# Weights loaded by pairs of column blocks, state added by VectorE, sums drawn into the sets: three edits to an mLSTM and Fourier-mix kernel

## The chip, the core and the metric

The kernel runs on one core of a Trainium2 chip. Its engines are TensorE (PE; its weight loads are shown apart as PEld), VectorE (DVE), ScalarE (ACT), GpSimd (POOL) and SyncE (SP), whose queue issues all of this kernel's DMAs. Every engine runs its own instructions in the order in which they were written, and waits on semaphores for the others. The metric is device time in microseconds of one execution; the profile is that of one further execution.

## The reference

Two stages follow each other. The first is an mLSTM cell over 4 batches, 8 heads, 768 tokens and head size 40; the second takes its output as x of shape (4, 768, 320), mixes it with a Fourier transform, and puts it through an MLP of width 1280.

```python
for t in range(S):
    m_new = np.maximum(f_gate[:, :, t] + m, i_gate[:, :, t])
    f_stab = np.exp(f_gate[:, :, t] + m - m_new)
    i_stab = np.exp(i_gate[:, :, t] - m_new)
    C = f_stab * C + i_stab * outer(v_t, k_t)
    n = f_stab * n + i_stab * k_t
    y[:, :, t] = sigmoid(o_t) * (C @ q_t) / max(|n . q_t|, 1)
...
u = x + np.real(fft(fft(x, axis=1), axis=2))
un = (u - mean(u)) / sqrt(var(u) + 1e-6)
out = u + np.maximum(un @ w_ch1, 0.0) @ w_ch2
```

The two weight arrays come as float64 and are turned into float32 on the chip.

## The kernel before

**mLSTM.** A batch is cut into 6 chunks of 128 tokens. Within a chunk the recurrence becomes matrix products: scores of keys and queries (`mlstm_scores`, L465, into the two banks `ps`, of which there is one pair), weighed by DVE with a matrix of exponentials (`mlstm_weigh`, L471; ACT makes the exponentials in `mlstm_exp`, L421), then the output of the chunk (`mlstm_from_chunk`, L486) on top of what the state gives (`mlstm_from_state`, L479, from C and the scaled queries qg). The state itself: `mlstm_to_state` (L496) forms what the chunk adds, in the PSUM tile `pc`; `mlstm_decay` (L455, POOL) shrinks the old state with `decB`; `mlstm_gather` puts the new state into `C_next`, and copies the chunk's output to `hT` by ACT (L517 to L528). PE turns that to tokens (`mlstm_turn`, L535), and `mlstm_finish` (L544 to L550, DVE) divides and gates it: x. In batches 1 to 3 the shrunk state lies in `C_next` and DVE adds `pc` to it (L515; a copy, L513, for chunk 0). In batch 0 the shrunk state lies in a tile of its own, `Cd`; PE adds it to `pc` by a product with the identity (L501), and ACT copies the sum (L511). The decays of batch 0 come from DVE (`dec`, L293) by a product (L297) and a copy (L301).

**Mix.** `mix_fold` and `mix_seq` (L695, L698) transform along the tokens, `mix_feat` (L729, into `pu`) along the features, `mix_add` (L749) adds to x, `mix_center` (L765, ACT) subtracts the mean, `mix_turn` (L772, PE, into `put`) turns it, and `mix_turn_out` (L777, ACT) writes the MLP's input `uT`.

**MLP.** The hidden layer has 10 column blocks of 128, two to a step. Batch 0 is plain: `mlp_in` (L837, L841, into `pm`), `mlp_relu` (L850, ACT), `mlp_out` (L943). Batches 1 to 3 use Strassen-Winograd schemes of seven products: `mlp_block` (L897, L902; five blocks of four steps; ACT copies at L915 to L924, DVE adds at L906, relu at L932 and L936) and `mlp_out_pair` (L999; three pairs of token blocks, called sets of four steps), which needs the sums S1 to S4 of hidden blocks (`hidden_sums`, L985, DVE) and adds its results to the output (`residual`, L949, DVE). The two banks x and y of a pair are those that the last adds of `mlp_block`, or the pair before, have just read.

**Weights.** Each of the 10 pieces of 640 columns goes through four steps: `load` (SP, L334, into one of two `raw` buffers), `take` (DVE, L344 and L346: exponent and mantissa), `convert` (ACT, L351 and L352), `join` (DVE, L358 to L364). A load waits until the join of the piece two before has freed its buffer, and what stands behind it in SP's queue waits with it. Of the first weights' five pieces two hold the first 128 input rows (columns 0 to 639 and 640 to 1279), two the last 128 rows, and one, `w1t_sb`, the 64 rows between.

**Order.** Nothing is scheduled by a planner: each step is entered by hand under a slot and a phase, and the steps are written out sorted by both:

```python
def at(slot, phase, fn, *args):
    plan.setdefault((slot, phase), []).append((fn, args))
EVAC, FILL, MAIN, FILL_PE = range(4)
```

Batch 0's mLSTM begins at slot 0 with three slots a chunk, its mix at 22, its MLP at 31; batch 1's mLSTM begins at 32. `when` gives the slots of take, convert and join for each piece, `early` those of the loads.

Of the kernel before, what the change touches and what calls it, by code (L numbers as in the profile page):

```python
# [19 lines left out]
L = 128  # L20
# [30 lines left out]
def kernel(  # L51
# [51 lines left out]
    h_first = const.tile([L, NP, 1], FP, name="h_first")  # L103
    w1_sb = const.tile([L, 2, DFF], FP, name="w1_sb")
    w1t_sb = const.tile([L, DFF // 2], FP, name="w1t_sb")
    w2_sb = const.tile([L, NFF, DM], FP, name="w2_sb")
# [4 lines left out]
    x_bufs = [const.tile([L, NT, DM + 2], FP, name=f"x{n}") for n in range(2)]  # L111

    s_last = const.tile([L, NFF // 2 * L], FP, name="s_last")
    Cd_bufs = [s_last[:, n * NP * D1:(n + 1) * NP * D1].rearrange("p (n m) -> p n m", m=D1) for n in range(2)]
    hT_bufs = [const.tile([L, NP, L], FP, name=f"h{n}") for n in range(2)]
# [6 lines left out]
    def at(slot, phase, fn, *args):  # L122
        plan.setdefault((slot, phase), []).append((fn, args))
# [16 lines left out]
    def gates(gp):  # L140
# [41 lines left out]
        mlstm_load(0, 2)  # L182
        w1_pieces[1].load()
        for t in hT_bufs + Cd_bufs:
            nc.gpsimd.memset(t, 0.0)
# [134 lines left out]
    class Piece:  # L320
# [33 lines left out]
        def join(self):  # L354
# [7 lines left out]
            for d in self.dst:  # L362
# [3 lines left out]

    part = 2 * DM
    w1_pieces = [Piece([w1_sb[:, f // 2, f % 2 * part:(f % 2 + 1) * part]], w_ch1[:, f * part:(f + 1) * part])
                 for f in (0, 2, 1, 3)]
    w1_pieces.insert(2, Piece([w1t_sb], w_ch1[:, 4 * part:]))  # L370
    w2_flat = w_ch2.rearrange("p f m -> p (f m)")
# [74 lines left out]
    def mlstm_decay(b, c):  # L446

        k = chunks[b, c]
        if 0 < c < NT - 1:
            if b == 0:  # L450
                k.Cd = Cd_bufs[c % 2]
            for hip in range(2):
                r, m = slice(hip * 64, hip * 64 + D), slice(hip * 64, hip * 64 + D1)
                d = decB[r, b * NP:(b + 1) * NP, c].unsqueeze(2).to_broadcast([D, NP, D1])
                nc.gpsimd.tensor_tensor(out=k.Cd[r] if b == 0 else k.C_next[r, :, m], in0=k.C[r, :, m], in1=d,  # L455
                                        op=OP.mult)

# [31 lines left out]
    def mlstm_to_state(b, c):  # L489
        k = chunks[b, c]  # L490
        if c < NT - 1:
            add = b == 0 and c > 0
            k.pc = ps_h.tile([L, NP, D1], FP, name="pc", tag="ph")
            for h in range(H):
                r0 = (h % 2) * 64
                nc.tensor.matmul(k.pc[r0:r0 + D, h // 2, :], k.kn[:, h, :], k.vw[:, h, :], start=(h < 2), stop=not add,  # L496
                                 skip_group_check=True)
            if add:
                for hip in range(2):
                    r = slice(hip * 64, hip * 64 + D)  # L500
                    nc.tensor.matmul(k.pc[r], ident[:, r], k.Cd, start=False, stop=True, skip_group_check=True)  # L501

    def mlstm_gather(b, c):
        k = chunks[b, c]
        k.hT = hT_bufs[(b * NT + c) % 2]
        if c < NT - 1:
            for hip in range(2):
                r, m = slice(hip * 64, hip * 64 + D), slice(hip * 64, hip * 64 + D1)
                Cv = k.C_next[r, :, m]
                if b == 0:  # L510
                    nc.scalar.copy(out=Cv, in_=k.pc[r])  # L511
                elif c == 0:
                    nc.vector.tensor_copy(out=Cv, in_=k.pc[r])  # L513
                else:
                    nc.vector.tensor_tensor(out=Cv, in0=Cv, in1=k.pc[r], op=OP.add)  # L515
        if c in BACKWARDS:
            nc.scalar.copy(out=k.hT[:, :, 1:], in_=backwards(k.ph, L - 1, L - 1))  # L517
            if c > TG:
                nc.scalar.copy(out=k.hT[:, :, 0:1], in_=k.ph[:, :, 0:1])
            else:  # L520
                nc.gpsimd.tensor_copy(out=k.hT[:, :, 0:1], in_=h_first)
# [306 lines left out]
    def mlp_in(b, gr, f):  # L828


        k = mixes[b]
        u = [uT_bufs[gr][:, ch].rearrange("p c t -> p (c t)") for ch in range(3)]
        if f % 2 == 0:
            k.pm = [bank("pm", [L, TG * L]) for _ in range(2)]
        for i, ch in ((1, 1),) if f % 2 else ((0, 0), (0, 1), (1, 0)):
            f0 = (f // 2 * 2 + i) * L
            nc.tensor.matmul(k.pm[i], w1_sb[:, ch, f0:f0 + L], u[2 * ch], start=(ch == 0), stop=False)  # L837
        if f % 2:
            for i in range(2):
                r = slice(i * TAIL, (i + 1) * TAIL)  # L840
                nc.tensor.matmul(k.pm[i], w1t_sb[r, f // 2 * L:(f // 2 + 1) * L], u[1][r], start=False, stop=True)  # L841

# [12 lines left out]
    def block(t, n):  # L855
        return t[:, n * L:(n + 1) * L]
# [3 lines left out]
    def weight_sums(n):  # L860

        w = w1_sb.rearrange("p c (n two t) -> p c two n t", two=2, t=L)
        if n == 0:
# [9 lines left out]
        out, x, y, op = ((S3, w[:, 0, 0], w[:, 0, 1], OP.subtract), (w[:, 0, 1], w[:, 0, 1], w[:, 1, 1], OP.add),  # L873
                         (S2, w[:, 0, 1], w[:, 0, 0], OP.subtract), (S4, w[:, 1, 0], S2, OP.subtract))[n]
# [12 lines left out]
    def mlp_block(b, i, step):  # L887
# [5 lines left out]
        T2, T3, T4 = w1x["T"]  # L893
        A = {(r, ch): block(w1_sb[:, ch], f + r) for r in range(2) for ch in range(2)}

# [3 lines left out]
        def tails(gr, banks):  # L899
            for r, bank in enumerate(banks):  # L900
                rows = slice(r * TAIL, (r + 1) * TAIL)
                nc.tensor.matmul(bank, block(w1t_sb, i)[rows], mlp_u(gr, 1)[rows], start=False, stop=True,  # L902
                                 skip_group_check=True)
# [83 lines left out]
    def mlp_out_pair(b, n, step):  # L987
# [8 lines left out]

        def product(po, a, w, start=False):
            for f in range(half):
                nc.tensor.matmul(po, a[:, f], w[:, f], start=start and f == 0, stop=f == half - 1, skip_group_check=True)  # L999
# [4 lines left out]
        if step == 0:  # L1004
            product(x, pair_block(n, 1, 1), w[0, 0], True)
            residual(b, c1, first, x)
            product(y, pair_block(n, 1, 0), w[1, 0], True)
            residual(b, c1, first, y)
# [18 lines left out]
    def plan_mlp(b, s):  # L1027
# [15 lines left out]
        if b > 0:  # L1043
            for j in range(1, 5):
                at(s - 1, FILL + 0.3 if j < 3 else FILL_PE + 0.3, hidden_sums, 0, (j,), 0, NFF // 2 - 1)
            at(s, EVAC, hidden_sums, 0, (1, 2, 3, 4), NFF // 2 - 1, NFF // 2)
        for n in range(TG) if b > 0 else ():
# [63 lines left out]
    for s, load, c in early:  # L1111
# [66 lines left out]
def _pack_w1(w):  # L1178

    t = w[L:L + TAIL].reshape(TAIL, NFF // 2, 2, L).transpose(2, 0, 1, 3).reshape(L, DFF // 2)  # L1180
    return np.ascontiguousarray(np.concatenate([w[0:L], w[L + TAIL:], t], axis=1))

# [45 lines left out]
```

## Time and profile before

| | us |
|---|---|
| median of 3 runs | 422.78 (422.35 to 424.34) |
| profiled execution | 422.23 |
| its span | 420.5 |
| PE busy | 408.1 (97%) |
| DVE busy | 287.5 (68%) |
| ACT busy | 189.6 (45%) |
| POOL busy | 112.0 (27%) |

Times in the text count from the start of the span. A line of the timeline gives start, length, engine, line of the code, operation and tiles (out<-in), how many instructions are merged into it, and in brackets how long the engine had stood idle and what ended that. In the table of waits, a line gives who waited for whom, the sum, how often, and the longest. In the answer on stretches the columns are busy time of PE, PEld, DVE, ACT and POOL, PE's granted clock, the share of the DMA engines and GB/s. The granted clock is 1.00 throughout.

### The profile page before, as it was taken

How to read it: one execution, taken by the hardware profiler on the slowest of the kernel's cores; microseconds unless marked ns; L12 is line 12 of the kernel's file. 1: busy time of each engine (PE TensorE's matmuls, PEld its weight loads, DVE VectorE, ACT ScalarE, POOL GpSimd, SP SyncE). 2: the span in 40 equal slices, each digit the busy share in tenths (PEclk: the TensorE clock that was granted, in tenths of full speed). 3: DMA queues.
4: the chain of work that ended last, by engine and by line, in shares of the span. 5: the costliest groups of instructions: out<-in, count | busy, mean ns of one | idle time of the engine just before them, and what ended most of it. 6: DMA issues, size and time to landing. Idle time of an engine off the chain costs nothing.

```text
span 420.5 us, 7995 instructions
## 1 busy us (share of the span) xinstructions
PE 408.1 (97%) x2966; PEld 301.8 (72%) x2966; DVE 287.5 (68%) x682; ACT 189.6 (45%) x493; POOL 112.0 (27%) x194
## 2 busy tenths in 40 slices
PE   8999999999999999999999999999999999999997
PEld 6877555566567778776559998976459898455996
DVE  8798885767985647778646669778654786325552
ACT  6986375586561232654455423654451123455000
POOL 5554201468332421351221520440300000020000
PEclk9999999999999999999999999999999999999999
DMA  7889297657764254266000543300000000000010
GB/s 228 287 249 335 83 270 234 195 191 203 238 178 146 65 150 145 70 198 215 30 0 2 176 148 124 114 15 1 0 2 0 33 33 32 0 2 0 16 48 31
DMA packets 20549, 47.14 MB, mean 112 GB/s; under 512 B 2784, under 2 KB 9312, under 8 KB 20384
## 3 DMA queue, kind: packets, MB, share of 16 engines
q1 hardware_dynamic: 20512, 46.65, 35.6%
q8 instruction: 23, 0.38, 0.4%
q14 instruction: 14, 0.11, 0.1%
HBM read 42.52 MB, written 4.11 MB: 111 GB/s over the span
## 4 chain that ended last, share of the span: by engine, by line
PE 77%; DVE 12%; DMA 7%; ACT 2%; issue 1%; POOL 0%; SPq 0%; DVEq 0%; ACTq 0%
PE pm L897 17%; PE po L999 16%; PE po L943 8%; PE ps L465 5%; PE pm L902 5%; PE ph L486 5%; PE ph L479 4%; DMA kvt<-in_kv 3%; PE pm L837 3%; PE pu L729 3%; DVE S L985 2%; PE px L535 2%; DMA qk<-in_qkT 2%; PE pz L698 2%; PE put L772 1%; DVE x L949 1%
## 5 line engine op out<-in xcount | busy, mean ns | idle before, releaser
L949 DVE SCALAR_TENSOR_TENSOR x<-po,rstd,x 128x160 f32<-128x160 f32 (+1 forms) x69 | 27.0, 394 | 41.6 <-PE po L999 35.0
L906 DVE TENSOR_TENSOR h<-h,pm 128x384 f32<-128x384 f32 x60 | 30.5, 550 | 33.1 <-ACT h L919 24.7
L421 ACT ACTIVATE W<-W,colT 128x128 f32<-128x128 f32 x144 | 45.0, 395 | 0.0
L443 POOL TENSOR_SCALAR_AFFINE_SELECT W<-W 128x1024 f32<-128x1024 f32 x18 | 21.3, 1185 | 80.8 <-ACT W L421 42.5
L943 PE MATMUL po<-w_sb,h 128*128 128x320 f32 x120 | 34.4, 435 | 0.0
L471 DVE TENSOR_TENSOR W<-ps,W 128x512 f32<-128x512 f32 x48 | 30.7, 680 | 4.5 <-POOL W L443 4.3
L897 PE MATMUL pm<-uT,w_sb 128*128 128x384 f32 x90 | 32.8, 492 | 0.2 <-DVE uT L885 0.2
L837 PE MATMUL pm<-uT,w_sb 128*128 128x384 f32 x80 | 29.9, 501 | 0.7 <-DVE x L749 0.5
L777 ACT COPY uT<-put 128x384 f32<-128x384 f32 x24 | 11.2, 478 | 40.1 <-PE put L772 40.1
L943 PEld LDWEIGHTS po<-w_sb,h 128*128 128x128 f32 x120 | 22.3, 190 | 9.4 <-issue 0.8
L999 PE MATMUL po<-T,S 128*128 128x160 f32 x180 | 27.9, 302 | 0.7 <-DVE x L949 0.6
L465 PE MATMUL ps<-qk 40*128 40x128 f32 x384 | 27.8, 284 | 0.0
L999 PE MATMUL po<-w_sb,h 128*128 128x160 f32 x180 | 26.2, 301 | 1.2 <-DVE h L906 1.2
L999 PEld LDWEIGHTS po<-T,S 128*128 128x128 f32 x180 | 25.5, 190 | 2.6 <-DVE x L949 1.7
L792 POOL TENSOR_TENSOR t<-rstd 128x6 f32<-128x6 f32 x12 | 2.9, 244 | 90.3 <-DVE v L790 89.7
L999 PEld LDWEIGHTS po<-w_sb,h 128*128 128x128 f32 x180 | 24.9, 190 | 2.8 <-DVE h L906 2.4
L465 PEld LDWEIGHTS ps<-qk 40*128 40x128 f32 x384 | 23.4, 188 | 4.1 <-issue 0.7
L486 PE MATMUL ph<-W,kvt 128*41 128x128 f32 x384 | 25.8, 277 | 0.0
L524 ACT COPY h<-ph 41x512 f32<-41x512 f32 (+1 forms) x16 | 9.3, 582 | 35.5 <-PE ph L486 35.4
L431 POOL TENSOR_TENSOR qg<-qk,Gb 128x512 f32<-128x512 f32 x18 | 25.0, 1388 | 0.1
L479 PEld LDWEIGHTS ph<-qg,C 128*128 128x128 f32 x160 | 20.0, 192 | 6.2 <-issue 2.1
L897 PEld LDWEIGHTS pm<-uT,w_sb 128*128 128x128 f32 x90 | 16.2, 190 | 10.8 <-DVE h L906 1.5
(207 smaller groups left out, 862.2 us busy)
## 6 DMA issues: line engine op xcount, KB each, us to landing
W<-M_d SPq DMA_DIRECT2D x18, 512.0 KB
kvt<-in_kv SPq DMA_DIRECT2D x24, 324.0 KB
qk<-in_qkT SPq DMA_DIRECT2D x48, 160.0 KB
raw<-in_w SPq DMA_DIRECT2D x10, 640.0 KB
Gb<-G_d SPq DMA_DIRECT2D x36, 128.0 KB
so<-in_o SPq DMA_DIRECT2D x24, 160.0 KB
out<-x SPq DMA_DIRECT2D x24, 160.0 KB
ds_sb<-in_dft_s SPq DMA_DIRECT2D x1, 1155.0 KB
```

The source lines that it names most:

```text
L421: nc.scalar.activation(out=k.W[:, h, :], in_=M, func=AF.Exp, scale=-1.0, bias=colT[:, c, 0, b * H + h:b * H + h + 1])
L431: nc.gpsimd.tensor_tensor(out=k.qg, in0=k.qk[:, 0], in1=k.Gb, op=OP.mult)
L465: nc.tensor.matmul(k.ps[hip][:, p, :], k.qk[r, 1, p, :], k.qk[r, 0, p, :], start=True, stop=True)
L471: nc.vector.tensor_tensor(out=Wv, in0=k.ps[hip], in1=Wv, op=OP.mult)
L479: nc.tensor.matmul(k.ph[:, p, :], k.C[:, p, :], k.qg[:, p, :], start=(p == 0), stop=False, skip_group_check=True)
L486: nc.tensor.matmul(k.ph[hip * 64:hip * 64 + D1, p, :], k.v1[:, 2 * p + hip, :], k.W[:, 2 * p + hip, :], start=(c == 0 and p == 0), stop=Tr ...
L837: nc.tensor.matmul(k.pm[i], w1_sb[:, ch, f0:f0 + L], u[2 * ch], start=(ch == 0), stop=False)
L897: nc.tensor.matmul(bank, w, u, start=start, stop=True, skip_group_check=True)
L906: nc.vector.tensor_tensor(out=h, in0=h, in1=bank, op=OP.add)
L943: nc.tensor.matmul(k.po, hidden(gr, f)[:, i * L:(i + 1) * L], w2_sb[:, f, :], start=(f == 0), stop=(f == NFF - 1))
L949: nc.vector.scalar_tensor_tensor(out=u, in0=po, scalar=k.rstd[:, c:c + 1], in1=u, op0=OP.mult, op1=OP.add)
L999: nc.tensor.matmul(po, a[:, f], w[:, f], start=start and f == 0, stop=f == half - 1, skip_group_check=True)
```

## The change

Three edits. First, the five pieces of the first weights are cut by pairs of column blocks: piece i holds all input rows for blocks 2i and 2i+1, so that step i of the MLP needs piece i alone. The second piece is loaded at slot 6 and no longer at the start, and the slots of the others move. Second, batch 0's state is kept as in the other batches: POOL shrinks it into `C_next` and DVE adds `pc`; the product with the identity, ACT's copies and the tiles `Cd` go. Third, the sums for the first pair of token blocks are made for three of five hidden blocks while `mlp_block` still runs, and for the other two afterwards, S3 and S4 after the first step of the pair; that step forms four products of x, two of y, the last of x, and the other three of y.

```diff
-    w1_sb = const.tile([L, 2, DFF], FP, name="w1_sb")
-    w1t_sb = const.tile([L, DFF // 2], FP, name="w1t_sb")
+    w1_sb = const.tile([L, NFF // 2, 5, L], FP, name="w1_sb")
...
-    Cd_bufs = [s_last[:, n * NP * D1:(n + 1) * NP * D1].rearrange("p (n m) -> p n m", m=D1) for n in range(2)]
...
-        w1_pieces[1].load()
-        for t in hT_bufs + Cd_bufs:
+        for t in hT_bufs:
             nc.gpsimd.memset(t, 0.0)
...
-    part = 2 * DM
-    w1_pieces = [Piece([w1_sb[:, f // 2, f % 2 * part:(f % 2 + 1) * part]], w_ch1[:, f * part:(f + 1) * part])
-                 for f in (0, 2, 1, 3)]
-    w1_pieces.insert(2, Piece([w1t_sb], w_ch1[:, 4 * part:]))
+    w1_pieces = [Piece([w1_sb[:, i].rearrange("p k t -> p (k t)")], w_ch1[:, i * 5 * L:(i + 1) * 5 * L])
+                 for i in range(NFF // 2)]
...
-            if b == 0:
-                k.Cd = Cd_bufs[c % 2]
...
-                nc.gpsimd.tensor_tensor(out=k.Cd[r] if b == 0 else k.C_next[r, :, m], in0=k.C[r, :, m], in1=d,
-                                        op=OP.mult)
+                nc.gpsimd.tensor_tensor(out=k.C_next[r, :, m], in0=k.C[r, :, m], in1=d, op=OP.mult)
...
-            add = b == 0 and c > 0
             k.pc = ps_h.tile([L, NP, D1], FP, name="pc", tag="ph")
...
-            if add:
-                for hip in range(2):
-                    r = slice(hip * 64, hip * 64 + D)
-                    nc.tensor.matmul(k.pc[r], ident[:, r], k.Cd, start=False, stop=True, skip_group_check=True)
...
-                if b == 0:
-                    nc.scalar.copy(out=Cv, in_=k.pc[r])
-                elif c == 0:
+                if c == 0:
                     nc.vector.tensor_copy(out=Cv, in_=k.pc[r])
                 else:
                     nc.vector.tensor_tensor(out=Cv, in0=Cv, in1=k.pc[r], op=OP.add)
...
-            nc.tensor.matmul(k.pm[i], w1_sb[:, ch, f0:f0 + L], u[2 * ch], start=(ch == 0), stop=False)
+            nc.tensor.matmul(k.pm[i], w1_sb[:, f // 2, 2 * ch + i], u[2 * ch], start=(ch == 0), stop=False)
...
-            product(x, pair_block(n, 1, 1), w[0, 0], True)
+            product(x, pair_block(n, 1, 1), w[0, 0], True, 0, half - 1)
+            product(y, pair_block(n, 1, 0), w[1, 0], True, 0, 2)
+            product(x, pair_block(n, 1, 1), w[0, 0], False, half - 1, half)
             residual(b, c1, first, x)
-            product(y, pair_block(n, 1, 0), w[1, 0], True)
+            product(y, pair_block(n, 1, 0), w[1, 0], False, 2, half)
             residual(b, c1, first, y)
...
-                at(s - 1, FILL + 0.3 if j < 3 else FILL_PE + 0.3, hidden_sums, 0, (j,), 0, NFF // 2 - 1)
-            at(s, EVAC, hidden_sums, 0, (1, 2, 3, 4), NFF // 2 - 1, NFF // 2)
+                at(s - (5, 4, 3, 3)[j - 1], FILL_PE + 0.3, hidden_sums, 0, (j,), 0, NFF // 2 - 2)
+            at(s, EVAC, hidden_sums, 0, (1, 2), NFF // 2 - 2, NFF // 2)
+            at(s, MAIN + 0.1, hidden_sums, 0, (3, 4), NFF // 2 - 2, NFF // 2)
...
-    when = [((2, 0.7), (4, 0.5), (6, 0.6)), ((6, 0.7), (7, 0.5), (8, 0.6)), ((11, 0.7), (13, 0.5), (22, 0.6))]
-    when += [((22, 0.7), (23, 0.7), (27, 0.6)), ((27, 0.7), (28, 0.7), (32, 0.6))]
-    when += [((s, 0.7), (s + 1, 0.7), (s + 2, 0.6)) for s in (33, 36, 39, 42, 45)]
+    when = [((2, 0.7), (4, 0.5), (6, 0.6)), ((11, 0.7), (13, 0.5), (22, 0.6)), ((22, 0.7), (23, 0.7), (27, 0.6)),
+            ((27, 0.7), (28, 0.7), (31, 0.6))]
+    when += [((s, 0.7), (s + 1, 0.7), (s + 2, 0.6)) for s in (31, 34, 37, 40, 43, 46)]
     pieces = w1_pieces + w2_pieces
     for n, (w, p) in enumerate(zip(when, pieces)):
-        if n > 4:
+        if n > 3:
             at(when[n - 2][2][0] + 1, FILL + 0.7, p.load)
...
-             (5, mlstm_load_decay, 4), (6, None, 2), (7, mlstm_load_o, 3), (7, mlstm_load, 5),
-             (11, mlstm_load_decay, 5), (11, None, 3), (11, mlstm_load_o, 4), (12, load_tables, None),
-             (14, mlstm_load_o, 5), (23, None, 4)]
+             (5, mlstm_load_decay, 4), (6, None, 1), (7, mlstm_load_o, 3), (7, mlstm_load, 5),
+             (11, mlstm_load_decay, 5), (11, None, 2), (11, mlstm_load_o, 4), (12, load_tables, None),
+             (14, mlstm_load_o, 5), (23, None, 3)]
```

In `mlp_block` and `weight_sums` only the way in which a block of `w1_sb` is addressed changes; the host's packing of the first weights follows the new cut.

More of the change, by code (lines that the diff above doesn't have):

```diff
@@ L495, in mlstm_to_state @@
                 r0 = (h % 2) * 64
-                nc.tensor.matmul(k.pc[r0:r0 + D, h // 2, :], k.kn[:, h, :], k.vw[:, h, :], start=(h < 2), stop=not add,
+                nc.tensor.matmul(k.pc[r0:r0 + D, h // 2, :], k.kn[:, h, :], k.vw[:, h, :], start=(h < 2), stop=True,
                                  skip_group_check=True)
-            if add:
-                for hip in range(2):
-                    r = slice(hip * 64, hip * 64 + D)
-                    nc.tensor.matmul(k.pc[r], ident[:, r], k.Cd, start=False, stop=True, skip_group_check=True)
     def mlstm_gather(b, c):
@@ L835, in mlp_in @@
         for i, ch in ((1, 1),) if f % 2 else ((0, 0), (0, 1), (1, 0)):
-            f0 = (f // 2 * 2 + i) * L
-            nc.tensor.matmul(k.pm[i], w1_sb[:, ch, f0:f0 + L], u[2 * ch], start=(ch == 0), stop=False)
+            nc.tensor.matmul(k.pm[i], w1_sb[:, f // 2, 2 * ch + i], u[2 * ch], start=(ch == 0), stop=False)
         if f % 2:
@@ L840, in mlp_in @@
                 r = slice(i * TAIL, (i + 1) * TAIL)
-                nc.tensor.matmul(k.pm[i], w1t_sb[r, f // 2 * L:(f // 2 + 1) * L], u[1][r], start=False, stop=True)
+                nc.tensor.matmul(k.pm[i], w1_sb[r, f // 2, 4], u[1][r], start=False, stop=True)
     hid = {}
@@ L860, in weight_sums @@
     def weight_sums(n):
-        w = w1_sb.rearrange("p c (n two t) -> p c two n t", two=2, t=L)
+        A11, A21, A12, A22 = (w1_sb[:, :, j] for j in range(4))
         if n == 0:
@@ L872, in weight_sums @@
         S2, S3, S4 = (view(w1x[t]) for t in ("S2", "S3", "S4"))
-        out, x, y, op = ((S3, w[:, 0, 0], w[:, 0, 1], OP.subtract), (w[:, 0, 1], w[:, 0, 1], w[:, 1, 1], OP.add),
-                         (S2, w[:, 0, 1], w[:, 0, 0], OP.subtract), (S4, w[:, 1, 0], S2, OP.subtract))[n]
+        out, x, y, op = ((S3, A11, A21, OP.subtract), (A21, A21, A22, OP.add), (S2, A21, A11, OP.subtract),
+                         (S4, A12, S2, OP.subtract))[n]
         nc.vector.tensor_tensor(out=out, in0=x, in1=y, op=op)
@@ L893, in mlp_block @@
         T2, T3, T4 = w1x["T"]
-        A = {(r, ch): block(w1_sb[:, ch], f + r) for r in range(2) for ch in range(2)}
+        A = {(r, ch): w1_sb[:, i, 2 * ch + r] for r in range(2) for ch in range(2)}
         def product(bank, w, u, start=False):
@@ L901, in tails @@
                 rows = slice(r * TAIL, (r + 1) * TAIL)
-                nc.tensor.matmul(bank, block(w1t_sb, i)[rows], mlp_u(gr, 1)[rows], start=False, stop=True,
+                nc.tensor.matmul(bank, w1_sb[rows, i, 4], mlp_u(gr, 1)[rows], start=False, stop=True,
                                  skip_group_check=True)
@@ L995, in mlp_out_pair, with product @@
         w = {(r, side): w2_sb[:, 1 - r:NFF:2, side * HALF_D:(side + 1) * HALF_D] for r in range(2) for side in range(2)}
-        def product(po, a, w, start=False):
-            for f in range(half):
+        def product(po, a, w, start=False, f0=0, f1=half):
+            for f in range(f0, f1):
                 nc.tensor.matmul(po, a[:, f], w[:, f], start=start and f == 0, stop=f == half - 1, skip_group_check=True)
@@ L1178, in _pack_w1 @@
 def _pack_w1(w):
-    t = w[L:L + TAIL].reshape(TAIL, NFF // 2, 2, L).transpose(2, 0, 1, 3).reshape(L, DFF // 2)
-    return np.ascontiguousarray(np.concatenate([w[0:L], w[L + TAIL:], t], axis=1))
+    t = w[L:L + TAIL].reshape(TAIL, NFF // 2, 2, L).transpose(2, 0, 1, 3).reshape(L, NFF // 2, L)
+    a, z = (r.reshape(L, NFF // 2, 2 * L) for r in (w[0:L], w[L + TAIL:]))
+    return np.ascontiguousarray(np.concatenate([a, z, t], axis=2).reshape(L, -1))
 def _pack_w2(w):
```

## The prediction

> **What bounds the kernel now.** I read the engine table first, then the waits of all engines, then the timelines of the three places that the diff touches. All times below are the profiled execution's own: span 420.5 us, 422.23 us as timed, 0.55 us under the median of 422.78 us.
>
> ```profile
> PE 408.1 (97%) x2966; PEld 301.8 (72%) x2966; DVE 287.5 (68%) x682; ACT 189.6 (45%) x493; POOL 112.0 (27%) x194
> ```
>
> TensorE (PE) is idle for 12 us in all, so a gain has to be PE work taken out or one of its few waits; a loss is any wait put ahead of PE. Who waits (engine, line, releaser: us, times, longest):
>
> ```profile
> DVE e L344 <- DMA raw<-in_w: 6.4, 2, 5.3
> ...
> PE po L999 <- DVE h L906: 1.2, 2, 0.6
> PE ph L479 <- POOL eo L618: 0.8, 1, 0.8
> ...
> SPq L334 <- DVE m L360: 13.4, 3, 12.5
> ```
>
> PE's own waits are below 1 us each. The other two lines matter more: the queue of loads (SP) once stands still 12.5 us until a weight buffer is free, and VectorE (DVE) once stands 5.3 us for a piece of weights. Today that costs PE nothing. Timeline of that place (start, us, engine):
>
> ```profile
> 49.51 0.33 SPq L334 DMA_DIRECT2D raw<-in_w  x1
> ...
> 59.19 0.53 SPq L334 DMA_DIRECT2D raw<-in_w  x1
> ...
> 61.14 0.87 ACT L850 ACTIVATE h<-pm 128x384 f32<-128x384 f32 x2
> ...
> 63.06 0.61 ACT L765 ACTIVATE uc<-x 128x384 f32<-128x384 f32 x1
> ...
> 63.97 0.49 PE L772 MATMUL put<-ident,uc 128*128 128x128 f32 x3
> ...
> 67.56 0.49 DVE L344 TENSOR_SCALAR e<-raw 128x640 uint32<-128x640 uint32 x1 [5.34 <-DMA raw<-in_w]
> ...
> 68.08 0.83 ACT L351 ACTIVATE e<-e,ebias 128x640 uint32<-128x640 uint32 x1 [3.11 <-DVE e L344]
> ```
>
> The piece issued at 59.19 lands at 67.5. ScalarE (ACT) waits for it too, but only after it has done the relu (L850) and the centering (L765) that PE's transpose at 63.97 needs. The queue was full:
>
> ```profile
> 49.50:67.50 18.00, 17.19 (x80) 9.87 (x78) 11.49 (x23) 11.06 (x24) 1.80 (x2) 1.00 0.95 269
> ```
>
> (last two: DMA share 0.95, 269 GB/s). The other two places:
>
> ```profile
> 37.92 0.48 PE L496 MATMUL pc<-vw,kvt 128*40 128x41 f32 x16
> ...
> 39.49 1.13 PE L479 MATMUL ph<-qg,C 128*128 128x128 f32 x8 [0.81 <-POOL eo L618]
> ...
> 38.43 1.28 DVE L471 TENSOR_TENSOR W<-ps,W 128x512 f32<-128x512 f32 x2
> ...
> 386.78 1.48 DVE L906 TENSOR_TENSOR h<-h,pm 128x384 f32<-128x384 f32 x3
> ...
> 387.38 2.98 PE L999 MATMUL po<-w_sb,h 128*128 128x160 f32 x20 [0.57 <-DVE h L906]
> ...
> 390.74 1.63 PE L999 MATMUL po<-T,S 128*128 128x160 f32 x10 [0.38 <-DVE x L949]
> ```
>
> **Part A, state of the first batch.** Removed: 16 identity records (L501) on PE. From 21.35 to 21.73 such a step takes 0.38, so 4 x 0.38 = 1.5 us. ACT loses its 10 copies (L511, 0.29 each), so its copies of h come 0.6 us earlier and PE's two waits for them at L535 (0.40 and 0.39) go. That is 2.3 us, if nothing else is late. Added on DVE: 10 copies or adds; L513 and L515 show 0.33 and 0.32 for the same shape, about 0.70 a pair. DVE is in order, so their place decides:
>
> - Chunk 0: the pair stands ahead of qg (L429, now 14.65) and dec (L293), and waits until pc (L496) ends at 15.15. It ends at 15.9, qg at 16.5, dec at 16.77 instead of 15.51; PE waits for dec at L297: 16.83 instead of 15.57, +1.26.
> - Chunks 1 to 3: PE makes this up: 1.26 - 3 x 0.38 - 0.79 puts pc of chunk 3 near 32.0 instead of 32.29. DVE now idles for pc (done 32.5), adds until 33.2, and weighs chunk 4 (L471, 1.25) until 34.5. PE, ready at 33.8 for the scores of chunk 5 (L465), needs those buffers: 34.55 against 34.45 before.
> - Chunk 4: behind that weighing stand three finishes (L544 to L550, from 33.16 to 38.43 today, 4.9 to 5.3), the weighing of chunk 5 (1.2) and only then the add of chunk 4 (0.7). 34.5 + 5.1 + 1.2 + 0.7 = 41.5. PE needs that state at L479, today at 39.49: 41.6, **+2.1**.
>
> What follows on PE (L486, L535, then the sequence transform) is back to back, so 2.1 stays; DVE's join before 50 us, and with it the release of SP, moves by the same. Bounds: +0.5, if the three finishes overlap PE's delay better than I place them, to +2.8, with the collision on every finish.
>
> **Part B, weights by pairs.** Pieces are 640 columns as before; one load moves from the start to slot 6, and every later piece is one step behind in number. The piece issued at slot 28 was the sixth, taken at slot 33. It becomes the fifth, with take, convert and join at 31, 32, 33. SP's order before it from slot 23 on is the same, and the hold until the join of slot 22 too, so it lands where the sixth did: at 67.5 (A's shift moves all of it alike and is left out here). New waits: DVE stands at its take from 62.2, as before; behind it are now the join and only then weighing and residual input. ACT stands at its convert, and this convert stands ahead of the first relu pair (L850), four exponentials and the centering (L765). PE's put (L772) waits for the centering:
>
> take 67.56; ACT converts 68.08 to 69.54 (0.83 and 0.72); relu pair to 70.35; exponentials 1.27 to 71.55; centering 0.61 to 72.1. PE's put starts at 72.1 instead of 63.97: **8.2 us** during which PE has nothing else, as its queue is in order.
>
> Second wait: before, the next join stood ahead of the copy of C (L513); now it stands behind it and ahead of the add at L749. After pc near 81.1: copy 0.7, join 2.4, two row copies 0.7, add 0.5: 85.4. PE's product at 76.32, which waits for that add (0.52 today), would be ready at 83.4 and starts at 85.5, 9.2 later than before. So B is **+9.2**. I find no other wait up to 122 us: each weighing is done 1 to 10 us ahead of its scores, and the 0.74 at L479 (109.8) may go or stay. Bounds: 18.0 us x 269/335 (the page's best slice) would land the piece 3.6 earlier, leaving 4.6; without any give-back it is 8.2 + 2.1 = 10.3. I take 9.2, since the same load in the same queue was measured.
>
> [...]
>
> **Part C, sums in the sets.** The four sums (L985) now cover three blocks early and two late, the same elements. Of the early ones S1 and S2, until now ahead of the last three adds (L906, 386.78), move two and more steps up, where DVE waits for ACT's copies (24.7 us of such waits in all). The first add releases PE's first product, so the 0.57 goes, for batch 2 (314.19) and batch 3 (387.38); batch 1 has scores in between and gains nothing. The wait at 390.74 remains: the relus end near 388.65, S1 and S2 for two blocks take some 0.43 each (one block 0.29, four 0.69), the residual 0.38, so PE starts near 390.1: 0.64 in batch 3, 0.57 of it the same wait. In the pairs after, y starts after four instead of five products, 398.57 instead of 398.83, while its bank is free at 398.84: 0.27 waited, but the next step waits for DVE until 400.57 today anyway, so nothing is lost. Sum 0.57 + 0.64 = **-1.2**. Bounds: -1.9, if the other 0.6 of L949 goes too, to +1.6, if all six later pairs lose 0.27.
>
> **Sum.** 422.2 + 2.1 + 9.2 - 1.2 = 432.3 as profiled, 432.9 against the median.
>
> **The rivals.**
> 1. *Faster.* PE work taken out is what counts, and the covers hold: the piece lands by about 61 us, and DVE gets its adds done between other work. Then 422.8 - 1.5 - 0.8 - 1.2 = 419.3. For it: PE is busy 97%, and the first batch is PE's. Against: the measured landing at 67.5, ahead of which there is no slack at all. It decides if the convert ends before PE asks at 63.97, a landing 8 us earlier. 10%.
> 2. *About the same.* Only A and C act: 422.8 + 2.1 - 1.2 = 423.7. For it: in the program before, ACT's wait at 68.08 was harmless. Against: the relu and the centering were ahead of it. 7%.
> 3. *Half.* The load lands at the best rate, 4.6: 428.3. 8%.
> 4. *Sums gain nothing* (what the change says of the sets is not seen by PE): 434.1. Inside the range, counted with the forecast.
> 5. *Worse.* The backlog of joins on DVE reaches the second layer of the first batch, whose weights are all due at 122: one more wait of join and add, 3 to 6 us: 437 to 439. 5%.
>
> **The numbers.** The forecast has 70%. The range goes from rival 3 with A at its low bound (422.8 + 0.5 + 4.6 - 1.9 = 426.0, less the 0.7 of L479: 425.3) to 422.8 + 2.8 + 10.3 + 1.6 = 437.5: 425.3 to 437.0. No change that a measurement of this kernel can tell is about 0.5%, 2.1 us. Faster 0.10 (rival 1), same 0.07 (rival 2), slower 0.83.
>
> **What would show it.** A: no L501, DVE adds with waits for pc, L479 of chunk 5 waiting over 2 us for one. B: PE's put waits about 8 us for the centering, ACT stands at its convert from 61 on with the relu behind it. C: no wait at the first L999 of batches 2 and 3. Wrong if PE has no wait over 3 us before 90 us.

## The result, and the profile after

The changed kernel takes 442.73 us (median of 4 runs, 441.49 to 445.02) where the kernel before takes 422.99 us (422.35 to 424.34) beside it: ratio 1.0469, 95% interval 1.0411 to 1.0526, or +19.8 us. The forecast was 432.9 us, 425.3 to 437.0. The direction was right, and so were the places; the size was half of it. The profiled execution is the longest of the four: 445.02 us, span 443.3, 22.8 more than before.

The engine table of the changed kernel, and TensorE's granted clock in 40 slices of the span (tenths of full speed; before, every slice had a 9):

```profile
PE 417.7 (94%) x2950; PEld 309.2 (70%) x2950; DVE 290.5 (66%) x692; ACT 186.6 (42%) x483; POOL 113.3 (26%) x192
...
PEclk9898997779998999999999999999999999999999
```

TensorE has 16 instructions fewer and is busy 9.6 us longer. The second line says why: the same work was done at a lower clock, 0.50 by the stretches below, in five places. The waits of TensorE (engine, line, releaser: us, times, longest):

```profile
PE put L757 <- ACT uc L750: 10.0, 5, 8.8
PE pm L821 <- DVE x L734: 2.8, 1, 2.8
PE pd L294 <- DVE dec L290: 1.7, 1, 1.7
PE ph L471 <- DVE x L535: 1.6, 1, 1.6
...
PE ph L471 <- POOL qg L426: 1.0, 1, 1.0
PE ph L471 <- DVE C L500: 0.9, 1, 0.9
...
PE po L983 <- DVE x L933: 0.6, 2, 0.3
```

Before, each of TensorE's waits was under 1 us (0.8 at most), apart from the start. Of the new ones those of 8.8, 2.8, 1.7 and 0.9 us were forecast at their places (the last with over 2 us), those of 1.6 and 1.0 us were not, and the wait of `po` for the hidden block that part C was to remove is gone. Timeline of the place with the 8.8 us (start, us, engine, and in brackets the idle time before it and its releaser):

```profile
63.60 0.53 SPq L331 DMA_DIRECT2D raw<-in_w  x1
...
72.37 0.49 DVE L341 TENSOR_SCALAR e<-raw 128x640 uint32<-128x640 uint32 x1 [6.23 <-DMA raw<-in_w]
...
72.90 0.83 ACT L348 ACTIVATE e<-e,ebias 128x640 uint32<-128x640 uint32 x1 [7.95 <-DVE e L341]
...
74.26 0.85 ACT L834 ACTIVATE h<-pm 128x384 f32<-128x384 f32 x2
75.00 1.27 ACT L416 ACTIVATE W<-W,colT 128x128 f32<-128x128 f32 x4
76.17 0.61 ACT L750 ACTIVATE uc<-x 128x384 f32<-128x384 f32 x1
...
76.83 0.90 PE L757 MATMUL put<-ident,uc 128*128 128x128 f32 x3 [8.77 <-ACT uc L750]
...
80.52 2.51 PE L714 MATMUL pu<-dd_sb,Z 128*128 128x321 f32 x4
```

The chain is the one foretold, link by link: the load lands late, ScalarE stands at the convert, and relu, exponentials, centering and `put` stand behind it. What was not foretold is in the durations of the last two lines. Three transposes take 0.90 where they took 0.49, and four products of the feature transform 2.51 where they took 1.35. The stretches of the same execution (bounds, us, then busy us of PE, PEld, DVE, ACT and POOL with their instructions; the last three numbers are the granted clock, the DMA share and GB/s):

```profile
14.81:18.22 3.41, 1.74 (x30) 1.22 (x26) 2.39 (x7) 3.35 (x7) 0.65 (x3) 1.00 0.41 125
18.22:21.63 3.41, 3.41 (x25) 3.06 (x24) 1.89 (x3) 1.99 (x8) 1.49 (x5) 0.50 0.92 258
...
72.40:82.60 10.20, 5.77 (x13) 3.03 (x14) 5.34 (x9) 6.33 (x17) 1.80 (x2) 0.52 0.52 160
82.60:92.90 10.30, 8.46 (x70) 4.80 (x69) 5.08 (x9) 6.22 (x16) 3.10 (x3) 0.98 0.18 52
92.90:99.70 6.80, 5.56 (x10) 2.70 (x12) 3.69 (x9) 2.96 (x7) 2.62 (x4) 0.53 0.53 155
```

The clock falls from 1.00 to 0.50 at 18.22 us, at 72.84 (until 83.08) and at 93.32 (until 100.14); the last three rows begin and end some 0.4 us early, so they read 0.52, 0.98 and 0.53. Two more such stretches of 3.4 us begin at 38.70 and 134.28: the second behind the wait of 1.6 us, the first behind two of 0.44 and 0.53 us that lie close together. Altogether some 27 us at half clock, and 27 x 0.5 / 443 is the 0.03 that the execution's mean clock of 0.969 lacks. The other three executions had mean clocks of 0.973 to 0.981.

**Ledger of the delay**, the start of landmarks on TensorE, after less before, in the two profiled executions:

| landmark | after - before | what came in |
|---|---|---|
| first product of the MLP (57.42 before) | +3.9 | part A |
| `put` (63.97) | +12.9 | 8.9: wait for the centering |
| product of the next pair (68.34) | +15.9 | 3.0: half clock |
| product that waits for the mix's add (76.32) | +17.8 | 1.9: longer wait for VectorE |
| state product, batch 1, chunk 1 (79.91) | +20.8 | 3.0: half clock |
| the same, chunk 4 (109.82) | +22.6 | 1.8: two waits of 1.0 and 1.6 |
| turn to tokens behind it (117.01) | +24.2 | 1.6: half clock |
| end of the span | +22.8 | -1.4: part C |

### The profile page after: what moved, and what is told of

It reads as the page before. It is cut to its first block, busy times and chain, and to the rows that moved or that the text cites. A ratio compares the mean times of both kernels' runs of the same rounds, so it can differ in the third digit from the quotient of the medians.

```text
span 443.3 us, 7963 instructions
## 1 busy us (share of the span) xinstructions
PE 417.7 (94%) x2950; PEld 309.2 (70%) x2950; DVE 290.5 (66%) x692; ACT 186.6 (42%) x483; POOL 113.3 (26%) x192
## 4 chain that ended last, share of the span: by engine, by line
PE 80%; DVE 12%; ACT 2%; DMA 2%; issue 2%; POOL 2%; ACTq 0%; DVEq 0%; POOLq 0%
PE po L983 17%; PE pm L881 16%; PE po L927 7%; PE pm L886 5%; PE ph L478 5%; PE ps L457 5%; PE ph L471 4%; PE pu L714 4%; PE pm L821 3%; DMA raw<-in_w 2%; PE put L757 2%; PE px L520 2%; PE pz L683 2%; PE pc L487 1%; PE pz L671 1%
## 5 line engine op out<-in xcount | busy, mean ns | idle before, releaser
L821 PE MATMUL pm<-uT,w_sb 128*128 128x384 f32 x80 | 33.1, 547 | 2.9 <-DVE x L734 2.8
L881 PE MATMUL pm<-uT,w_sb 128*128 128x384 f32 x90 | 32.8, 492 | 0.2 <-DVE uT L869 0.2
L457 PE MATMUL ps<-qk 40*128 40x128 f32 x384 | 28.8, 286 | 0.6 <-PE pM L215 0.4
L478 PE MATMUL ph<-W,kvt 128*41 128x128 f32 x384 | 27.5, 289 | 0.0
L471 PEld LDWEIGHTS ph<-qg,C 128*128 128x128 f32 x160 | 21.2, 202 | 8.2 <-issue 3.9
L500 DVE TENSOR_TENSOR C<-C,pc 40x164 f32<-40x164 f32 x32 | 10.3, 322 | 25.3 <-PE pc L487 23.3
L471 PE MATMUL ph<-qg,C 128*128 128x128 f32 x160 | 23.1, 291 | 3.5 <-DVE x L535 1.6
```

The lines of the kernel that those rows point to most:

```text
L457: nc.tensor.matmul(k.ps[hip][:, p, :], k.qk[r, 1, p, :], k.qk[r, 0, p, :], start=True, stop=True)
L471: nc.tensor.matmul(k.ph[:, p, :], k.C[:, p, :], k.qg[:, p, :], start=(p == 0), stop=False, skip_group_check=True)
L478: nc.tensor.matmul(k.ph[hip * 64:hip * 64 + D1, p, :], k.v1[:, 2 * p + hip, :], k.W[:, 2 * p + hip, :], start=(c == 0 and p == 0), stop=Tr ...
L821: nc.tensor.matmul(k.pm[i], w1_sb[:, f // 2, 2 * ch + i], u[2 * ch], start=(ch == 0), stop=False)
L881: nc.tensor.matmul(bank, w, u, start=start, stop=True, skip_group_check=True)
```

## The experiments

Theory 1: direct waits, as the prediction has them, and behind the longer ones passages in which TensorE runs at half its clock, which the prediction lacks. Rivals: the late landing of the load is the cause wherever its convert stands; one part is harmless without the others; the clock falls for a reason other than TensorE's waits, or its fall costs nothing. All ratios are to the kernel before on the same chip (medians 423.6 to 424.2 us there).

**Each part alone.** Three kernels from the kernel before. Their edits are those of the diff; in short:

```diff
# e1_state
...
-                if b == 0:
-                    nc.scalar.copy(out=Cv, in_=k.pc[r])
-                elif c == 0:
+                if c == 0:
...
# e2_weights
...
-    when += [((s, 0.7), (s + 1, 0.7), (s + 2, 0.6)) for s in (33, 36, 39, 42, 45)]
+    when += [((s, 0.7), (s + 1, 0.7), (s + 2, 0.6)) for s in (31, 34, 37, 40, 43, 46)]
# e3_sums
...
-            at(s, EVAC, hidden_sums, 0, (1, 2, 3, 4), NFF // 2 - 1, NFF // 2)
+            at(s, EVAC, hidden_sums, 0, (1, 2), NFF // 2 - 2, NFF // 2)
+            at(s, MAIN + 0.1, hidden_sums, 0, (3, 4), NFF // 2 - 2, NFF // 2)
```

> The kernel before with the state of the first batch added by VectorE alone (part A). Theory 1 (waits, and behind each longer wait of PE a passage at half the granted clock): as in the profile after, pd waits some 1.7 us for dec and the products stand some 1 us for the add of chunk 4; two stretches of 3.4 us at half clock, near 18 and 38 us, which the profile before lacks; the landmark of the first pair of the MLP comes 3.9 us later, and the time is 422.9 + 3.9 = 426.8 us. The prediction's working (waits alone): + 2.1, 424.9 us. Rival (A costs nothing by itself, what follows in the weights is the root): 422.9 us within 0.5.

> The kernel before with the first weights loaded by pairs of column blocks alone (part B). Theory 1: put waits some 8 to 9 us for the centering, a stretch at half clock of about 10 us starts while it waits and a second one comes behind the wait of the first product for the mix's add; the time is 422.9 + 17 to + 20 = 440 to 443 us. The prediction's working (waits alone): + 9.2, 432.1 us. Rival (B's wait is mostly a sequel of A's delay): below 430 us.

> The kernel before with the sums of the first pair of token blocks put into the sets alone (part C). Theory 1: the waits ahead of the first products of the last MLP sets go, - 1.2 to - 1.4: 421.5 to 421.7 us, clock as before. Rival (in the changed kernel the sums gain nothing or cost): 422.9 us or up to 424.5.

| kernel | median us | ratio, 95% interval | us | forecast in the prediction |
|---|---|---|---|---|
| e1_state | 428.65 | 1.0108 [1.0079, 1.0137] | +4.6 | +2.1 |
| e2_weights | 438.68 | 1.0347 [1.0319, 1.0375] | +14.7 | +9.2 |
| e3_sums | 421.76 | 0.9947 [0.9932, 0.9963] | -2.2 | -1.2 |

The sum of the three is +17.1 us, the whole change +19.8; with their intervals that is no clear difference. So no part is a mere sequel of another. e2 came out below the 17 to 20 us that I expected. Its profile shows why: its waits are those of the changed kernel (8.4, 2.8 and 1.6 us), but only the first was followed by a passage at half clock, where in the changed kernel's profile all three were; the mean clocks of its four executions, 0.987 to 0.992, say the same of the others. e3 has the lowest ratio of this study.

e1's waits:

```profile
PE ph L475 <- DVE C L504: 2.4, 2, 2.1
PE ph L475 <- DVE den L533: 2.3, 1, 2.3
PE pd L296 <- DVE dec L292: 1.7, 1, 1.7
```

Three waits of 1.7, 2.1 and 2.3 us, of which only that of 2.1 us was followed by half a clock (from 43.33 us). The wait of `pd` was not, though it was as long as in the changed kernel. The bounds of the next rows lie whole multiples of 3.413 us ahead of 43.33:

```profile
16.03:19.44 3.41, 1.98 (x24) 1.56 (x26) 2.77 (x7) 3.35 (x9) 1.21 (x4) 1.00 0.60 186
19.44:22.85 3.41, 3.41 (x50) 3.00 (x48) 2.79 (x4) 1.35 (x6) 0.93 (x4) 1.00 0.96 234
```

Set beside 14.81 to 18.22 and 18.22 to 21.63 of the changed kernel: PE busy for 1.98 us of 3.4 here and 1.74 there, and then a clock of 1.00 here and 0.50 there. What the place of such stretches decides is taken up under "What stays open".

**The place of the converts.** The changed kernel with the steps of the fifth piece and all later ones two slots later, so that the convert stands behind relu and centering again:

```diff
-    when += [((s, 0.7), (s + 1, 0.7), (s + 2, 0.6)) for s in (31, 34, 37, 40, 43, 46)]
+    when += [((s, 0.7), (s + 1, 0.7), (s + 2, 0.6)) for s in (33, 36, 39, 42, 45, 48)]
```

> The changed kernel with taking, converting and joining the pieces from the fifth on two slots later (33, 36, 39, ... in place of 31, 34, 37, ...), loads as they follow from that. Theory 1 (the place of the convert on ScalarE, ahead of relu, exponentials and centering, makes put wait): put's wait and both stretches at half clock behind it go, - 15 to - 19, 424 to 428 us. Rival (the late landing of the load is the cause wherever its work stands): the wait moves to a later instruction and the time stays above 436 us.

Measured: 426.61 us, ratio 1.0070 [1.0046, 1.0093]. Some 17 of the 19.8 us are gone with one line. ScalarE and TensorE in its timeline:

```profile
66.81 0.61 ACT L750 ACTIVATE uc<-x 128x384 f32<-128x384 f32 x1
...
67.72 0.49 PE L757 MATMUL put<-ident,uc 128*128 128x128 f32 x3
...
71.98 0.83 ACT L348 ACTIVATE e<-e,ebias 128x640 uint32<-128x640 uint32 x1 [3.25 <-DVE e L341]
```

ScalarE still stands at that convert until 71.98, only 0.9 us earlier than in the changed kernel (72.90) and long after `put` asked. But the centering starts at 66.81, and `put` follows without a wait. The landing is nearly the same, the order on ScalarE decides: the rival of the load falls. The edit moves take and join on VectorE too, and the wait for the mix's add went with it (0.5 us, 2.8 in the changed kernel), so the 17 us are those of both orders.

**The clock by itself.** Idle products are put into TensorE's order just ahead of the late `put`, so that it has work while ScalarE stands; nothing reads them.

```diff
+    def busy(n):
+        pw = ps_h.tile([L, 2 * L], FP, name="pi", tag="ph")
+        for i in range(n):
+            nc.tensor.matmul(pw, rest[:, 0:L], rest, start=True, stop=True, skip_group_check=True)
+
+    at(33, FILL_PE + 4.9, busy, 34)   # e5_fill: 18
```

> The changed kernel with 34 idle products of 256 columns (0.235 us each, 8.0 us) on TensorE in the stretch in which put waits for the centering (8.77 us in the profile after); nothing else is changed and nothing reads them. Theory 1 (the granted clock halves because PE stands): put still starts near 76 us, but the stretch at half clock from 72.4 to 82.6 us is gone, and the 5.8 us of work behind put that lay in it take 2.9 us less: ratio about 1.040 where the changed kernel has 1.047. Rival (the clock falls for another reason, or the falling clock costs nothing): the stretch stays, no gain. Rival (the added products delay put): slower than 1.047.

Measured: 445.99 us, ratio 1.0502 [1.0443, 1.0562], which tells nothing of the clock, since I had mistaken the price of a product: the 0.235 us was my estimate, and the run showed 0.436; one is two instructions, and the 34 took 14.84 us, not 8.0, so `put` came 7 us late, at 84.07. The clock from 70 to 84 us was full (1.00). The dose mended:

> The changed kernel with 18 idle products in the stretch in which put waits (the run with 34 showed that one takes 0.436 us, so 18 take 7.9 us and end ahead of the centering; 34 had taken 14.8 us and held put back). Theory 1: put starts at the same time as in the changed kernel, the stretch at half clock around it is gone and the 5.8 us of work in it take 2.9 us less: ratio 1.037 to 1.042, where the changed kernel has 1.047. Rival (the clock falls for another reason or costs nothing): 1.047.

Measured: 440.26 us, ratio 1.0387 [1.0356, 1.0418], 3.5 us below the changed kernel's. Stretches and timeline of e5_fill:

```profile
72.40:82.60 10.20, 10.20 (x45) 6.95 (x45) 4.78 (x9) 6.29 (x17) 1.80 (x2) 1.00 0.49 147
90.90:94.40 3.50, 2.93 (x5) 1.75 (x6) 3.09 (x7) 1.54 (x3) 1.96 (x4) 0.57 0.47 85
```

```profile
69.41 7.93 PE L1107 MATMUL pi<-rest 128*128 128x256 f32 x36
77.18 0.49 PE L757 MATMUL put<-ident,uc 128*128 128x128 f32 x3
...
79.09 1.35 PE L714 MATMUL pu<-dd_sb,Z 128*128 128x321 f32 x4
...
91.47 4.47 PE L821 MATMUL pm<-uT,w_sb 128*128 128x384 f32 x8 [2.80 <-DVE x L734]
```

`put` comes no earlier (77.18 against 76.83), the wait has only been filled up to its end; but the clock is 1.00, `put` takes 0.49 again and the feature transform 1.35, and from `put` to the next pair's product it is 4.4 us in place of 7.4. Useless work made this place faster by 3.0 us. For the whole kernel the two intervals overlap a little (1.0411 and 1.0418), and its 3.5 us are not this passage alone, as others differ too: e5_fill's profile has none near 134 us, and one of 6.8 us from 43.61. The wait that was not filled, 2.8 us at 91.47, was followed by half a clock as before (0.57, and 4.47 us for what takes 2.8). In e4_late both waits and half clock were taken away; here the half clock alone.

**How long a wait it takes.** In the kernel before, the centering of the fifth token block is written several times, so that `put` (at 75.25 us there, waiting 0.28 us) waits longer:

```diff
+        for _ in range(3 if (b, c) == (0, ORDER[4]) else 1):   # e11_four: 5, e12_eight: 9
-        nc.scalar.activation(out=uc, in_=twice, func=AF.Identity, scale=-1.0, bias=u[:, DM:DM + 1])
+            nc.scalar.activation(out=uc, in_=twice, func=AF.Identity, scale=-1.0, bias=u[:, DM:DM + 1])
```

> The kernel before with the centering of the fifth token block of the first batch written three times in place of once on ScalarE (same values): put, which waits 0.28 us for it in the profile before, waits about 0.28 + 2 x 0.52 = 1.3 us; the 0.5 us that the next product waits for VectorE goes. Waits alone: + 0.5 us (ratio 1.001). With a passage at half clock behind it: + 2.2 us (1.005). Theory 1 expects no passage behind so short a wait.

> The same with five writings: put waits 0.28 + 4 x 0.52 = 2.4 us. Waits alone: + 1.6 us (ratio 1.004). Theory 1: a stretch of 3.4 us at half clock behind it in most executions, + 1.7 us more: + 3.3 us (1.008).

> The same with nine writings: put waits 0.28 + 8 x 0.52 = 4.4 us. Waits alone: + 3.7 us (ratio 1.009). Theory 1: one or two stretches of 3.4 us at half clock in every execution, in part over the wait itself: + 5 to + 6.5 us (1.012 to 1.015).

| kernel | wait of `put`, us | ratio, 95% interval | runs with a mean clock of 0.996 or less |
|---|---|---|---|
| e10_two | 1.57 | 1.0014 [0.9998, 1.0031] | 0 of 10 |
| e11_four | 2.87 | 1.0059 [1.0038, 1.0080] | 2 of 10 |
| e12_eight | 5.46 | 1.0146 [1.0110, 1.0181] | 4 of 4 |

A writing took 0.65 us, not the 0.52 that I had estimated, so the waits are longer than I planned. e10 and e12 are within what was expected; e11 is a miss, since I expected the passage in most executions and it was in two of ten. Those two are its longest, 427.77 and 427.81 us; the other eight lie at 424.84 to 427.14, near the price of the wait alone. e12's stretches, the second of them with the end of the wait (which ended at 81.56) and the work behind it:

```profile
74.00:78.00 4.00, 2.11 (x25) 0.90 (x20) 3.54 (x11) 3.71 (x7) 2.60 (x3) 1.00 0.39 131
78.00:84.70 6.70, 3.14 (x7) 2.05 (x8) 1.44 (x4) 5.54 (x11) 1.88 (x4) 0.53 0.65 190
```

**What the parts are worth when mended.** Three kernels: A alone with another order on VectorE (the copy of chunk 0's state behind the decay, the add of chunk 3 behind the weighing of chunk 4); B and C without A, with the later slots of e4; and all three parts with both.

```diff
# e9_order and e7_all: the state of batch 0 is added by a step of its own
...
+            at(s + 2, FILL + (0.02 if (b, c) == (0, 4) else 0), mlstm_decay, b, c)
+            if b == 0 and c < NT - 1:
+                at(*((4, FILL + 0.55), (7, FILL), (10, FILL), (14, FILL + 0.01), (16, FILL))[c], mlstm_add, b, c)
# e8_noA and e7_all: slots (33, 36, 39, 42, 45, 48) as in e4_late
```

> Part A alone, with the order on VectorE mended: the copy of chunk 0's state behind the decay that pd waits for, the add of chunk 3 behind the weighing of chunk 4. Theory 1 (A's cost is its order on VectorE, and the half clock behind the wait): the waits of pd and with it the half clock near 18 us go, 424.2 - 0.5 to + 1.5 us (ratio 0.999 to 1.0035), where A alone had 1.0108. Rival (the add on VectorE costs by its own 0.7 us a chunk and by PSUM being held longer): no better than 1.009.

> Parts B and C without A, with the pieces from the fifth on taken, converted and joined two slots later. From the runs so far, as a sum: C alone - 2.3, B at the late slots 426.6 - 424.2 - 4.4 + 2.3 = + 0.3: 422.2 us, ratio 0.995. Theory 1: no wait of PE over 1 us, clock 1.00 throughout. Rival (B costs something apart from the place of the converts): above 424.2 us.

> All three parts, with the later slots for the pieces from the fifth on and the mended order of the state on VectorE. Theory 1: C's - 2.3, the late B's + 0.3, and A with the mended order - 0.5 to + 1.5: 421.7 to 423.7 us, ratio 0.994 to 0.999. Rival (A costs as before): 1.007.

e9_order: 426.25 us, ratio 1.0056 [1.0029, 1.0083]. Half of A's 4.6 us is gone, less than I expected: `pd` waits 0.42 us as before, but the wait for the state of chunk 4 is as long as in e1 (2.1 us), as it still stands behind three finishes and the weighing of chunk 5 on VectorE. e8_noA: 422.97 us, ratio 0.9982 [0.9949, 1.0015]; I expected 0.995, so B at the late slots may cost 1.5 us, or nothing, by these intervals. e7_all: 424.69 us, ratio 1.0009 [0.9983, 1.0036], above the 0.994 to 0.999 expected: what e9 did not mend. None of the three beats e3.

e8 shows the clock once more, and a miss: I had expected no wait over 1 us and no passage. Nine of its ten executions ran with a mean clock of 1.00 and took 421.30 to 423.45 us; the tenth had 0.992 and took 427.2 us. That one is the profiled one. The stretch at half clock began at 113.22, at the end of a wait of 2.43 us (until 113.48):

```profile
108.00:112.70 4.70, 3.05 (x14) 1.45 (x10) 3.01 (x8) 2.61 (x6) 0.17 (x1) 1.00 0.95 326
112.70:119.60 6.90, 6.12 (x52) 5.57 (x54) 6.21 (x10) 2.08 (x8) 2.90 (x2) 0.54 0.33 112
```

## Why the prediction was right and where it was wrong

**Right: what bounds the kernel, and which waits come.** TensorE is busy nearly throughout (97% of the span before) and its order is fixed, so a wait ahead of it is lost as far as nothing behind it falls away. The prediction asked for a wait of about 8 us at `put`, with ScalarE at its convert and the relu behind it: 8.77 us, in that order. It asked for `pd` 1.26 us later: 16.88 in place of 15.57, +1.31. It said that the second wait for the mix's add would come, and that C would take away the wait of `po` for the hidden block. All were there, and so was the wait of over 3 us without which the prediction called itself wrong. Its weighing of the rate of the page's best slice (335 GB/s) against the one measured over the same load before (269 GB/s) also held: the piece issued at 63.60 was taken up at 72.37, 8.8 us later, where the one before had taken 8.4.

**Wrong: the sum priced the work behind the waits at the durations of the profile before.** Every term was a wait; the work that follows was assumed to be as quick as ever, and moved as a block. In the profile after, some 27 us of it ran at half clock. Of the delay at the landmarks above, 3.0 + 3.0 + 1.6 = 7.6 us lie in such passages from `put` on, and 1.7 us (half of the 3.4 us from 38.70) in A: 9.3 us of the 24.2 at the last landmark. That is the term the sum did not have. The waits came out larger too, 13.4 us for 10.1, but by themselves they would have ended near 436 us, inside the range. e5_fill takes one of these passages away without moving `put` forward, and 3.0 us go between `put` and the next pair's product.

Point by point:

| step | forecast | waits measured | half clock |
|---|---|---|---|
| A: state on VectorE | +2.1 (0.5 to 2.8) | +2.2 after, +2.9 in e1 | +1.7 |
| B: `put` behind the convert | +8.2 | +8.9 | +3.0 |
| B: wait for the mix's add | +1.0 | +1.9 | +3.0 |
| A or B: further waits up to 122 us | 0 | +1.8 | +1.6 |
| C: sums in the sets | -1.2 (-1.9 to +1.6) | -1.4 after, -2.2 in e3 | 0 |
| sum | +10.1 | +13.4 after | +9.3 |

*A.* The mechanism held; one link was misplaced. The prediction had VectorE idle for `pc` of chunk 3 and weighing chunk 4 from 33.2. In the changed kernel VectorE was never idle there: a finish and the take of a piece (0.9 us) stood ahead of the add, and the weighing began at 34.99:

```profile
33.07 0.49 DVE L535 TENSOR_TENSOR x<-px,so 128x320 f32<-128x320 f32 x1
33.48 0.48 DVE L341 TENSOR_SCALAR e<-raw 128x640 uint32<-128x640 uint32 x1
...
34.28 0.67 DVE L500 TENSOR_TENSOR C<-C,pc 40x164 f32<-40x164 f32 x2
34.99 1.29 DVE L463 TENSOR_TENSOR W<-ps,W 128x512 f32<-128x512 f32 x2
```

In e1 the state product of chunk 5 starts 3.5 us later than before, 0.6 of which it had at the first `pc` already: +2.9 for the waits, and by reckoning +1.7 for the half clock behind them; at the first `put` of the mix it is 4.5 us behind, the same 0.6 left out. That is near the 4.6 us that e1 lost by the medians, but its profile has the further wait of 2.3 us (0.7 before), so the parts do not add up to it exactly. The sign "waiting over 2 us" came in e1 (2.1 us) and not in the changed kernel (0.9 us), where `pc` itself came late, at half clock (41.87). The first passage there (18.2 to 21.6) left little: the delay of 2.9 us at the scores of chunk 2 had shrunk to 1.1 at the state product of chunk 3, with no wait of TensorE in between. Two slips of the working: 1.26 - 3 x 0.38 - 0.79 puts `pc` of chunk 3 near 31.6, the 32.0 belongs to two steps of 0.38; and the range's upper sum is 437.5, not 437.0.

*B.* The wait of `put` was estimated from the profile before within 0.7 us. The wait for the mix's add grew by 0.9 us more than reckoned, as the join ahead of it took 3.2 us (89.59 to 92.78) and not 2.4. The sentence "I find no other wait up to 122 us" failed: the scaled queries and a finish of batch 1 came 1.0 and 1.6 us late for the state products. The second place is not B's alone: it waits 2.3 us in e1 and 1.4 in e9, which have A only, and 0.6 to 1.2 us in the kernels with neither. I have not separated what made them late.

*C.* Right in its sign and near its size; alone it gained 2.2 us (1.6 to 2.9 by its interval).

*The rivals.* Faster, same and half rested on an earlier landing or harmless converts; the landing was as late as measured before. The rival for worse, 437 to 439 us by a backlog of joins, has the right side of the forecast but another mechanism, and is still too low. The bounds of the range came from the sizes of the waits alone, and the range made that way did not hold the result.

**What stays open.** The same wait brought a passage in one execution and none in the next, so its length alone does not decide. The profiles show more. The passages of one trace begin whole multiples of 3.413 us apart (in the changed kernel 6, 10, 6 and 12 of them from one to the next: 34 in the 116.06 us from 18.22 to 134.28), on a grid that lies elsewhere from profile to profile (its first bound behind the start is at 1.2 us in the changed kernel, at 2.4 in e1, 2.7 in e5_fill and 0.6 in e8). The wait of 2.8 us for the mix's add, on this grid, in the changed kernel:

```profile
89.90:93.32 3.42, 1.16 (x7) 0.31 (x4) 3.34 (x5) 2.78 (x8) 3.42 (x3) 1.00 0.40 139
93.32:100.14 6.82, 6.00 (x10) 3.03 (x12) 3.30 (x8) 2.54 (x5) 2.20 (x4) 0.50 0.60 181
```

and in e2:

```profile
84.25:87.66 3.41, 2.18 (x9) 0.78 (x9) 3.31 (x5) 2.74 (x7) 2.49 (x3) 1.00 0.49 154
87.66:91.07 3.41, 1.56 (x5) 1.06 (x6) 3.26 (x8) 2.11 (x6) 3.23 (x4) 1.00 0.07 28
91.07:94.49 3.42, 3.42 (x20) 1.95 (x20) 1.02 (x3) 1.45 (x2) 0.00 (x0) 1.00 0.83 243
```

In the first most of the wait fell into one cell of the grid, with TensorE busy for 1.16 us, and the clock fell to 0.50; in e2 it was divided between two, 2.18 and 1.56, and the clock stayed at 1.00. In the eleven profiles whose clock shows the grid, cells at full clock with 1.45 us or less of busy time were followed by half clock 11 times of 11, those with 1.5 to 2.3 us 6 times of 18, those with more never. If each product's time is counted by the first number of its form over 128 (40 over 128 for the scores), all 17 cells ahead of a passage hold 1.45 us or less, and of all others only one does (1.41). This is read from the profiles afterwards; no run was made to test it. It accounts for why e2, with the same waits, had fewer passages; how the 19.8 us of the whole divide from one execution to the next beyond that is left to the intervals.

## What to carry to other kernels

Where an engine works in a fixed order, look at what stands behind a step that may wait for a load: the landing was harmless as long as the convert stood behind the relu and the centering, and cost 17 us when it, and with it the join on VectorE, stood ahead. Price a new wait of TensorE at its own length and again at the work behind it: here a wait of 2.8 us and one of 8.8 us each cost 3 us more in the work behind them, though the same 2.8 us cost nothing more in e2. If such a wait can't be removed, products that nobody reads can hold the clock up: here 18 of them (7.93 us) in the wait of 8.8 us held it at 1.00, with a ratio of 1.0387 where the changed kernel has 1.0469. They have to end ahead of the wait's end: 34 of them (14.84 us) delayed `put` by 7 us, with a ratio of 1.0502.

## What the hardware showed that I had not expected

- The granted clock fell from 1.00 to 0.50 behind waits of TensorE, in stretches of about 3.4 us or multiples of it (3.4, 6.8 and 10.2 us in the trace of the changed kernel), and work in them took nearly twice as long (three transposes 0.90 us in place of 0.49, four products of the feature transform 2.51 in place of 1.35).
- Short waits were enough, but not always. In the profiles of this case, waits of 1.1 to 1.5 us were followed by half a clock once of 6 times, waits of 1.5 to 1.7 us 3 times of 10, waits of 2.1 to 2.9 us 8 times of 11, waits of 5.4 us and more 3 times of 3. The same wait of 1.67 or 1.68 us for `dec` was followed by one in the changed kernel and e4, and by none in e1 and both kernels with idle products: in the cell of the grid it fell into (see "What stays open"), TensorE was busy for 1.74 us in the first two and for 1.98 to 2.11 us in the others.
- An idle product of 256 columns is two instructions and took 0.436 us in a row of 34 (14.84 us), nearly twice what I had reckoned.
